# A linear-attention and feed-forward kernel on one core: another order of its steps from the 380th on

## The chip, the core and the metric

The kernel runs on one core of a Trainium2 chip. The core has five engines that run their own queues in order and wait for each other through semaphores: TensorE (PE, matrix products, written to PSUM), VectorE (DVE, elementwise work, scans and 32x32 block transposes), ScalarE (ACT, copies and activations), GpSimd (POOL) and SyncE (SP), whose queue issues all the DMAs here. The time is the device time of one execution in microseconds (us). Before the change it was 537.36 us, the median of three runs (537.22 to 537.84).

## The reference

A recurrent gated linear attention runs over 4 batches, 8 heads, 768 tokens and head dimension 48; its output, 3072 tokens of 384 values, goes through a feed-forward block with a hard-swish and a hidden width of 2048:

```python
for t in range(S):
    state = alpha[:, :, t, :, None] * state + np.einsum('bhd,bhe->bhde', k[:, :, t], v[:, :, t])
    y[:, :, t] = np.einsum('bhd,bhde->bhe', q[:, :, t], state)
x = y.transpose(0, 2, 1, 3).reshape(B * S, H * D)
h = x @ w_in
g = h * np.clip(h + 3.0, 0.0, 6.0) / 6.0
out = g @ w_out
```

## The kernel before, in words

**Attention.** The sequence is cut into 24 chunks of 128 tokens (six for each batch, numbered 0 to 23). For chunk j the steps load alpha, k, q and v (`la`, `lk`, `lq`, `lv`), bring alpha, k and q into the layout with channels on partitions (`ca`, `tk`, `tq`; from chunk 6 on a DVE block transpose of four loads, L286), run one scan backwards for the decay to the chunk's end with a reciprocal (`r`, L309) and one forwards (`p`, L320), and multiply k and q by them (`k`, `q`, L332). `sc` are the chunk's scores on PE (L346), `m` masks them on DVE in four operations (L356), `qa` lets ACT place q beside them (L366). From chunk 8 on k comes into the layout by token through DRAM: DVE turns blocks (`kt`, L391), four DMAs write them (`kw`, L396) and four read them back (`kr`, L404). `u` is k's product with v (PE, L429), `sm` adds it to the state on DVE in two halves (L437, L439), `st` decays the state on POOL (L409), and `sv` places the state beside v: two ACT copies (L419), or a POOL memset where a batch begins. `ya` and `yb` are the two halves of the output (PE, L455), and `cy` copies it to x (ACT, L464).

**Feed-forward.** Two chunks make a group of 256 tokens (0 to 11). From group 2 on the first layer is done by 20 products instead of 24, from sums of blocks: `xc` makes eleven sums of blocks of x (DVE, 128x128), `y` made the sums of the weights once (DVE, 128x512), `M.g.i` is product i (PE, four matrix products, L600), `n` copies a product from its PSUM bank to one of 16 SBUF slots (ACT, L606), and `o.g.o.0` and `o.g.o.1` put output o together on DVE (L537 to L541). `e` is the relu of the hard-swish (ACT, L494), `h` its end (DVE, L498). The second layer uses seven products instead of eight: `s` makes sums of halves of the hidden block (DVE, L647, L664), `P.g.i` is product i (PE, eight matrix products, L703), `K` keeps partial results (ACT, L682 and L709), `G` finishes a quarter of the output (two by ACT, L720, and two by DVE, L723; group 1 has three by DVE), and `O` stores it (L728). `z` are idle products. A trailing number of a step names the buffer: a PSUM bank, a slot or an output tile.

**What sets the order.** All the code runs under a manual schedule. One long string lists 1788 steps, and each step emits its instructions at once; so the string alone sets the order on every engine's queue. An engine waits at an instruction until what it reads is there and what it overwrites has been read, and everything behind it on that engine waits too. The products of one accumulating chain use the same PSUM bank, so that for example `M.g.12` may start only when `n.g.11` has copied that bank. The chunk's buffers alternate with j (two each for alpha, k, q and their results), and v has three.

```python
    def run(words):
        for word in words.split():
            name, *at = word.split(".")
            steps[name](*(int(x) for x in at))
```

Of the kernel before, what the change touches and what calls it, by code (L numbers as in the profile page):

```python
# [17 lines left out]
def kernel(  # L18
# [42 lines left out]
    G = 2  # L61
# [510 lines left out]
    for i in range(8):  # L572
        r, o = divmod(i, 3)
        spots.append(raws[r].rearrange("p n w -> p (n w)").bitcast(FP)[:, o * QB : (o + 1) * QB])
    xc = consts.tile([C, len(X_SUMS), C], FP, tag="xc")
# [178 lines left out]
    with tc.manual_schedule():  # L754
# [3 lines left out]
               dx.0 w.2 d2.2 kb.1.0 ck.1 lq.1 r.2 sm.0.1 st.1 tq.1.2 q.1 d3.2 z.0.3 d1.2 dx.2  # L758
               lv.1.1 u.1.3.1 sv.1.0 sm.1.0 p.2 sm.1.1 sc.1.0.2 m.1 ya.0.3 yb.0 cy.0 lq.2 w.1 d1.1
               tq.2.1 q.2 d4.2 lk.2 tk.2.3 k.2 fa.2.0 d4.0 st.2 sc.2.0.2 d2.1 d3.1 m.2 dx.1 d4.1  # L760
               qa.1.1 lk.3 la.3 ta.3.1 ca.3 la.4 fa.0.1 sv.1.1 w.3 r.3 ta.4.3 ca.4 r.4 tk.3.1 k.3
               kb.2.0 qa.1.0 d2.3 ya.1.2 yb.1 cy.1 fa.1.2 lq.3 ck.2 d1.3 p.3 d3.3 lv.2.2 u.2.3.2
               sm.2.0 d4.3 fb.2 tq.3.1 q.3 fb.1 qa.2.0 sm.2.1 sv.2.0 st.3 fr.0.2.0 fg.0.2 lk.4
               tk.4.0 sv.2.1 w.5 d2.5 k.4 d3.5 d1.5 qa.3.0 d4.5 qa.2.1 sc.3.1.3 m.3 w.6 d2.6 d1.6
               d3.6 d4.6 lv.3.0 lq.4 w.7 kb.3.2 fb.0 f.0.3.3 kb.4.0 ya.2.1 ck.3 u.3.3.2 sm.3.0
               fr.0.3.1 fg.0.3 fr.0.1.0 fg.0.1 qa.3.1 sv.3.0 sm.3.1 p.4 d2.7 sv.3.1 d1.7 d3.7 d4.7
               f.0.5.0 fr.0.5.1 fr.0.0.0 fg.0.5 fg.0.0 tq.4.3 ck.4 la.5 ta.5.2 f.0.6.3 ca.5 w.4
               d2.4 ya.3.0 yb.3 cy.3 fr.0.6.1 yb.2 cy.2 w.9 d2.9 q.4 qa.4.1 d1.4 d1.9 dx.4 la.6 w.8
               d3.4 r.5 lk.5 w.10 d3.9 p.5 ca.6 fg.0.6 d4.9 w.12 lq.5 lv.4.1 d2.8 d3.8 f.0.7.2 d1.8
               st.4 d4.8 d4.4 w.11 fr.0.7.0 fg.0.7 f.1.7.0 fr.1.7.1 fg.1.7 sc.4.0.2 m.4 f.1.1.1  # L770
               fr.1.1.0 fg.1.1 f.1.3.3 fr.1.3.1 d2.10 d1.10 tk.5.3 f.1.0.2 d2.12 d3.10 d4.10 w.13
               fg.1.3 fr.1.0.0 fg.1.0 k.5 d3.12 lq.6 f.1.6.0 f.1.2.1 u.4.1.0 sm.4.0 d1.12 d4.12
               sv.4.0 qa.4.0 ya.4.2 fr.1.6.1 fg.1.6 w.15 tq.5.3 fa.4.3 sv.4.1 d2.11 kb.5.1 d2.13
               fr.1.2.0 f.1.4.2 fr.1.4.1 d1.11 sm.4.1 q.5 r.6 d3.11 d3.13 fg.1.4 d4.11 lv.5.0 lk.6
               tq.6 p.6 d2.15 d3.15 fg.1.2 d1.13 d4.13 sc.5.0.3 yb.4 f.1.5.0 fr.1.5.1 fg.1.5 tk.6
               m.5 b.1.0.2 fb.4 b.1.1 d1.15 d4.15 st.5 y.5 w.14 la.7 lk.7 cy.4 d2.14 qa.5.1 ck.5
               b.0.0.1 fr.0.4.0 d3.14 k.6 q.6 ca.7 fg.0.4 d1.14 d4.14 x.0 y.1 y.10 b.0.1 y.0 y.2
               u.5.2 P.1.0.0 K.1.0 qa.5.0 sv.5.0 qa.6.1 P.1.1.3 b.0.2 b.1.2 kb.6.0 ya.5.3 y.6
               s.1.0.0 sm.5.0 sv.5.1 G.1.0.0 tk.7 s.1.1.1 s.1.2.3 x.1 yb.5 cy.5 b.1.3 sc.6.1.2
               lv.6.2 ck.6 u.6.3.0 s.1.3.2 x.2 P.1.2 b.0.3 K.1.1 y.7 s.1.4 s.1.5 y.11 y.3 r.7  # L780
               xc.2.1 x.3 y.4 y.8 xc.2.3 k.7 xc.2.0 xc.2.4 y.9 y.12 y.16 y.13 y.15 P.1.3.3 K.1.2
               P.1.4 bo.1 P.1.5 xc.2.5 G.1.1.1 P.1.6 y.14 y.17 y.19 xc.2.6 sm.6.0 G.1.2.2 y.20
               M.2.0.2 lv.12.1 la.8 O.1.1 O.1.0 ca.8 y.18 y.21 y.23 so.1 G.1.3.3 n.2.0.8 bo.0 lq.7
               lv.7.0 O.1.2 m.6 xc.2.2 xc.2.10 xc.2.7 tq.7 r.8 p.7 xc.2.8 sv.6.1 M.2.15.3 M.2.1
               kb.7.3 n.2.1.9 M.2.16 M.2.2 n.2.2.10 M.2.7.0 n.2.7.11 sm.6.1 xc.2.9 q.7 p.8 M.2.3
               M.2.4 n.2.4.12 M.2.8 o.2.0.0 M.2.5 n.2.5.13 qa.7.0 sv.6.0 st.7 lk.8 O.1.3 lq.8 lk.9
               la.9 la.10 tk.8 tq.8 lq.10 lq.9 ya.6.1 yb.6 M.2.9 z.1.3 M.2.18.1 o.2.1.0 e.2.1.1
               M.2.10 cy.6 ck.7 sc.7.0.2 u.7.1.3 n.2.10.14 M.2.11 qa.7.1 ca.9 la.11 y.22 M.2.6.2
               h.2.1 q.8 m.7 e.2.0.0 h.2.0 n.2.11.15 qa.6.0 n.2.18.10 qa.8.1 M.2.12 M.2.19
               n.2.12.12 M.2.13 sm.7.0 sv.7.1 r.9 k.8 o.2.3.0 sv.7.0 ya.7.0 y.24 o.2.5.0 n.2.13.12  # L790
               o.2.2.0 yb.7 cy.7 sc.8.1.2 xc.3.1 o.2.2.1 e.2.2.1 xc.3.3 o.2.3.1 M.2.14 xc.3.4
               xc.3.0 xc.3.5 o.2.4.0 xc.3.7 xc.3.6 o.2.6.0 P.2.0.1 M.3.0.2 M.2.17 h.2.2 o.2.6.1
               e.2.3.0 h.2.3 o.2.7.0 n.3.0.12 M.3.1 n.3.1.9 e.2.5.1 M.3.7.0 n.3.7.13 xc.3.8 o.2.7.1
               K.2.0.3 xc.3.2 kt.8 e.2.6.0 h.2.6 tk.9 M.3.2 n.3.2.10 e.2.4.0 P.2.1 h.2.4 h.2.5
               s.2.0.14 e.2.7.0 G.2.0.1 h.2.7 M.3.3 M.3.4 n.3.4.8 k.9 s.2.1.11 M.3.8 o.3.0.0 ca.10
               kt.9 P.2.3.3 s.2.2.15 s.2.3.14 lv.8.2 kw.8 kr.8 lk.10 sm.7.1 xc.3.9 M.3.5 n.3.5.11
               K.2.2 e.3.0.1 xc.3.10 M.3.9 o.3.1.0 P.2.2 K.2.1 u.8.0.3 M.3.18.2 s.2.5 M.3.10
               n.3.10.14 n.3.18.15 e.3.1.0 s.2.4 P.2.4 tq.9 h.3.0 st.8 sv.8.0 M.3.11 n.3.11.8 tk.10
               p.9 sm.8.0 q.9 r.10 k.10 qa.9.0 qa.9.1 m.8 sm.8.1 h.3.1 M.3.19 o.3.5.0 kt.10 P.2.5
               G.2.2.0 st.9 M.3.12 sc.9.0.1 qa.8.0 n.3.12.10 o.3.3.0 kw.9 lv.9.0 kr.9 sv.8.1  # L800
               u.9.2.3 sm.9.0 sv.9.1 sv.9.0 G.2.1.2 sm.9.1 st.10 M.3.15.2 M.3.16 M.3.6.3 M.3.13 m.9
               o.3.4.0 o.3.6.0 tq.10 n.3.13.10 o.3.2.0 e.3.4.1 ya.8.2 yb.8 ya.9.3 yb.9 cy.9 M.3.14
               M.3.17 cy.8 xc.4.1 P.2.6 e.3.5.0 G.2.3.3 o.3.2.1 xc.4.3 h.3.4 xc.4.4 o.3.6.1 xc.4.5
               xc.4.0 xc.4.6 e.3.2.1 M.4.0.0 n.4.0.10 P.3.0.1 xc.4.7 o.3.7.0 p.10 h.3.5 o.3.3.1
               xc.4.8 M.4.7.3 M.4.1 xc.4.2 h.3.2 o.3.7.1 K.3.0.2 lk.11 O.2.2 tk.11 e.3.6.0 e.3.3.1
               h.3.3 P.3.1 e.3.7.1 n.4.1.13 M.4.2 ca.11 q.10 h.3.6 r.11 k.11 h.3.7 n.4.7.15 lv.10.2
               lv.11.0 kw.10 sc.10.0.1 kr.10 G.3.0.0 u.10.3.2 sm.10.0 qa.10.1 n.4.2.14 M.4.3 M.4.4
               M.4.8 s.3.0.9 xc.4.9 s.3.2.12 s.3.1.11 P.3.3.2 n.4.4.8 M.4.5 o.4.0.0 e.4.0.0 sv.10.1
               sm.10.1 xc.4.10 kt.11 O.2.0 O.2.3 lq.11 m.10 s.3.3.9 s.3.5 M.4.9 o.4.1.0 P.3.2
               sv.10.0 st.11 n.4.5.11 K.3.2 la.13 M.4.18.0 p.11 tq.11 lk.12 tk.12 K.3.1 M.4.10  # L810
               n.4.10.9 q.11 qa.10.0 n.4.18.12 e.4.1.1 la.12 s.3.4 ca.12 h.4.0 r.12 P.3.5 G.3.2.1
               h.4.1 M.4.11 P.3.4 n.4.11.8 M.4.12 n.4.12.14 qa.11.0 M.4.19 p.12 G.3.1.3 lq.12 kw.11
               O.2.1 tq.12 kr.11 u.11.3 sc.11.0.2 sv.11.0 O.3.1 lk.13 P.3.6 qa.11.1 M.4.6.2 G.3.3.2
               k.12 o.4.3.0 m.11 sm.11.0 sv.11.1 kt.12 M.4.13 n.4.13.14 q.12 o.4.3.1 e.4.3.0
               o.4.2.0 o.4.6.0 h.4.3 o.4.2.1 ya.10.1 ya.11.0 yb.10 yb.11 cy.11 cy.10 xc.5.1 ca.13
               xc.5.3 M.4.15.1 M.4.16 M.4.14 P.4.0.2 o.4.4.0 M.4.17 xc.5.4 o.4.5.0 xc.5.0 xc.5.5
               M.5.0.0 o.4.6.1 K.4.0.3 e.4.2.1 h.4.2 P.4.1 qa.12.1 e.4.4.0 xc.5.6 o.4.7.0 h.4.4
               o.4.7.1 tk.13 n.5.0.14 M.5.1 e.4.7.1 h.4.7 e.4.5.0 xc.5.2 h.4.5 xc.5.7 G.4.0.3
               e.4.6.1 h.4.6 s.4.1.12 s.4.0.11 xc.5.8 r.13 xc.5.9 xc.5.10 k.13 kw.12 kr.12 la.14
               sc.12.2.3 u.12.0.1 sm.12.0 n.5.1.13 M.5.2 n.5.2.15 M.5.7.1 n.5.7.8 P.4.3.3 s.4.2.9  # L820
               kt.13 lk.14 lq.13 O.3.0 O.3.3 lv.13.2 kw.13 O.4.0 lq.14 tq.13 lq.15 M.5.3 M.5.4
               M.5.8 s.4.3.10 P.4.2 sv.12.1 n.5.4.11 o.5.0.0 e.5.0.0 K.4.2 s.4.5 p.13 ca.14 M.5.9
               M.5.5 n.5.5.12 m.12 sm.12.1 o.5.1.0 q.13 P.4.5 K.4.1 G.4.2.0 qa.12.0 qa.18.0 s.4.4
               h.5.0 M.5.18.0 n.5.18.9 o.5.6.0 tk.14 qa.13.0 M.5.10 n.5.10.10 M.5.15.3 M.5.16
               M.5.11 M.5.19 r.14 k.14 n.5.11.11 o.5.7.0 kr.13 u.13.0.2 sc.13.1.3 M.5.12 P.4.4
               e.5.1.1 n.5.12.9 M.5.13 h.5.1 o.5.4.0 m.13 o.5.5.0 st.13 sv.13.0 ya.13.1 qa.13.1
               e.5.4.0 n.5.13.15 sm.13.0 sv.13.1 h.5.4 la.15 ca.15 sv.12.0 ya.12.3 yb.12 cy.12
               yb.13 cy.13 kt.14 G.4.1.2 tq.14 M.5.14 o.5.6.1 M.5.6.0 xc.6.1 o.5.3.0 xc.6.3 o.5.2.0
# [110 lines left out]
```

## Time and profile before

| | before |
|---|---|
| median of 3 runs | 537.36 us |
| the profiled execution | 537.71 us, of which its span is 535.56 us |
| PE busy, matrix products / weight loads | 523.6 us (98%) / 497.0 us (93%) |
| DVE busy | 475.1 us (89%) |
| ACT busy | 259.7 us (48%) |
| POOL busy | 50.4 us (9%) |
| granted TensorE clock | 1.00 |

The span runs from the first to the last instruction; the rest of the execution's time lies around it. Matrix products are pipelined, and the ends of their records are modelled, so PE's busy share alone doesn't say how full PE is; the distance from one start to the next does. DVE's records overlap by a little where one follows another without a wait. A wait is put down to the engine whose signal came last. In a timeline line the columns are the start, the length, the engine, the line of the kernel, the operation, what is written and read, how many instructions are merged, and in brackets the idle time ahead of it with what ended it. In a line of busy times by stretch the length is followed by the busy time of PE, of its weight loads, of DVE, ACT and POOL with their instruction counts, the granted clock, the share of the DMA engines and GB/s.

### The profile page before, as it was taken

What the parts mean: (1) busy time and instruction counts of PE and PEld (TensorE: products, weight loads), DVE (VectorE), ACT (ScalarE), POOL (GpSimd) and SP (SyncE); (2) the same over time, 40 slices, a digit from 0 to 9 for tenths busy, and PEclk for the clock granted to TensorE, in tenths of its full rate; (3) what the DMA queues carried; (4) which work ended last, traced back from release to release, by engine and by line L of the source; (5) the groups of instructions that cost most, each with busy time, mean ns of one, the idle gap of its engine ahead of it and who ended that gap; (6) DMA issues with size and microseconds to landing.
All of it is one profiled execution on the core that took longest, in us unless ns stands there. A gap on an engine that the chain in (4) does not pass through costs nothing.

```text
span 535.6 us, 15166 instructions
## 1 busy us (share of the span) xinstructions
PE 523.6 (98%) x6306; PEld 497.0 (93%) x6306; DVE 475.1 (89%) x839; ACT 259.7 (48%) x513; POOL 50.4 (9%) x71
## 2 busy tenths in 40 slices
PE   7799999999999999999999999999999999999997
PEld 7698886789999999999999999999999999999996
DVE  6999989999999899989999899999999898595381
ACT  3889864302753644543644444642634545553240
POOL 5333435000000000000010000000000000000000
PEclk9999999999999999999999999999999999999999
DMA  9998877006515155254354355055354042100001
GB/s 175 214 250 263 205 218 164 9 1 162 151 28 121 29 120 134 51 139 90 92 118 104 89 122 141 20 126 124 85 137 103 17 97 48 43 3 1 15 16 37
DMA packets 124100, 54.40 MB, mean 102 GB/s; under 512 B 83328, under 2 KB 116864, under 8 KB 124032
## 3 DMA queue, kind: packets, MB, share of 16 engines
q1 hardware_dynamic: 124032, 53.44, 42.4%
q8 instruction: 49, 0.80, 0.7%
q14 instruction: 19, 0.16, 0.1%
HBM read 44.50 MB, written 8.91 MB: 100 GB/s over the span
## 4 chain that ended last, share of the span: by engine, by line
PE 64%; DVE 20%; SPq 5%; DMA 3%; issue 3%; ACT 2%; POOL 2%; DVEq 0%; ACTq 0%; POOLq 0%
PE m_ps L703 28%; PE m_ps L600 24%; PE m_ps L478 4%; SPq L262 3%; PE t_ps L455 3%; DVE R L309 2%; DVE g_sb L498 2%; DVE A L356 2%; DMA v<-in_v_dram 1%; PE t_ps L346 1%; PE m_ps L516 1%; PE t_ps L429 1%; DVE g_sb L537 1%; DVE q L332 1%; DVE t L286 1%
## 5 line engine op out<-in xcount | busy, mean ns | idle before, releaser
L703 PE MATMUL m_ps<-w,g_sb 128*128 128x192 f32 x704 | 122.1, 327 | 0.7 <-ACT m_ps L709 0.6
L606 ACT COPY g_sb<-m_ps 128x512 f32<-128x512 f32 x110 | 63.5, 584 | 113.8 <-PE m_ps L600 97.4
L703 PEld LDWEIGHTS m_ps<-w,g_sb 128*128 128x128 f32 x704 | 113.7, 190 | 1.8 <-ACT m_ps L709 0.9
L703 PE MATMUL m_ps<-rings,g_sb 128*128 128x192 f32 x528 | 91.6, 327 | 0.6 <-ACT u L682 0.6
L703 PEld LDWEIGHTS m_ps<-rings,g_sb 128*128 128x128 f32 x528 | 85.3, 190 | 1.0 <-ACT u L682 0.9
L600 PE MATMUL m_ps<-xc,w 128*128 128x128 f32 x640 | 82.8, 277 | 0.5 <-DVE w L541 0.5
L600 PEld LDWEIGHTS m_ps<-xc,w 128*128 128x128 f32 x640 | 77.5, 192 | 1.7 <-issue 0.6
L494 ACT ACTIVATE r<-g_sb,half 128x512 f32<-128x512 f32 x80 | 56.7, 722 | 29.5 <-DVE g_sb L541 11.7
L498 DVE SCALAR_TENSOR_TENSOR g_sb<-r,g_sb 128x512 f32<-128x512 f32 x80 | 53.6, 683 | 7.2 <-ACT r L494 6.8
L600 PE MATMUL m_ps<-xT,raw 128*128 128x128 f32 x400 | 52.6, 278 | 1.0 <-ACT g_sb L606 0.9
L600 PEld LDWEIGHTS m_ps<-xT,raw 128*128 128x128 f32 x400 | 48.6, 192 | 2.0 <-ACT g_sb L606 1.4
L409 POOL TENSOR_TENSOR st<-sm,R 128x192 f32<-128x192 f32 x20 | 12.9, 644 | 354.4 <-DVE sm L439 305.6
L647 DVE TENSOR_TENSOR g_sb<-g_sb 128x512 f32<-128x512 f32 (+1 forms) x55 | 42.0, 792 | 1.4 <-PE m_ps L703 1.1
L600 PE MATMUL m_ps<-xT,w 128*128 128x128 f32 x320 | 42.0, 276 | 0.0
L600 PEld LDWEIGHTS m_ps<-xT,w 128*128 128x128 f32 x320 | 39.3, 192 | 0.1
L366 ACT COPY A<-q 48x256 f32<-48x256 f32 x88 | 35.6, 404 | 4.9 <-DVE q L332 3.7
L356 DVE TENSOR_TENSOR A<-t_ps,mask 64x256 f32<-64x256 f32 x96 | 36.0, 413 | 0.4
L478 PE MATMUL m_ps<-xT,w 128*128 128x256 f32 x144 | 32.8, 382 | 0.1
L600 PE MATMUL m_ps<-xc,raw 128*128 128x128 f32 x240 | 31.8, 276 | 0.0
L309 DVE TENSOR_TENSOR_SCAN R<-t,ones 128x516 f32<-128x516 f32 x24 | 29.6, 1235 | 1.1 <-ACT t L300 1.0
L478 PEld LDWEIGHTS m_ps<-xT,w 128*128 128x128 f32 x144 | 26.7, 190 | 3.8 <-POOL w L217 0.2
L600 PEld LDWEIGHTS m_ps<-xc,raw 128*128 128x128 f32 x240 | 29.6, 192 | 0.1
(105 smaller groups left out, 724.8 us busy)
## 6 DMA issues: line engine op xcount, KB each, us to landing
raw<-in_moe_w_out_dram SPq DMA_DIRECT2D x8, 768.0 KB, 5.2
raw<-in_moe_w_in_dram SPq DMA_DIRECT2D x6, 768.0 KB, 6.7
v<-in_v_dram SPq DMA_DIRECT2D x48, 96.0 KB, 3.0
out_dram<-oh SPq DMA_DIRECT2D x44, 96.0 KB, 1.7
far<-kq SPq DMA_DIRECT2D x64, 64.0 KB, 2.2
kb<-far SPq DMA_DIRECT2D x64, 64.0 KB, 2.0
aq<-in_alpha_dram SPq DMA_DIRECT2D x36, 96.0 KB, 2.4
qq<-in_q_dram SPq DMA_DIRECT2D x36, 96.0 KB, 2.4
```

What stands on the lines that cost most here:

```text
L262: nc.sync.dma_start(out=to[BLK * o : BLK * (o + 1), :, 0 : V * D - skip], in_=t[o // 2, :, :, skip : V * D])
L309: nc.vector.tensor_tensor_scan(out=reverse(R, n - 1, n), data0=reverse(ax, n, n), data1=reverse(ones, n, n), initial=0.0, op0=ALU.mult, op ...
L356: nc.vector.tensor_tensor(out=to[:, a], in0=sc[a][half], in1=mask[half, half].unsqueeze(1).to_broadcast([HB, NP, HB]), op=ALU.mult)
L366: nc.scalar.copy(out=to[:, a], in_=Q_t[j][64 * a : 64 * a + D, :, half])
L455: nc.tensor.matmul(y_of(j, (i + 1) // 2, p)[:, HB * b : HB * b + HB], vb[:, p, e : e + 32], A_t[j][:, b, 2 * p + a], start=(b == 0 and i = ...
L478: nc.tensor.matmul(h[:, f], w1[:, kk, o : o + C], xT_t[g][:, kk], start=(kk == 0), stop=(kk == KT - 1))
L494: nc.scalar.activation(out=to, in_=h, func=AF.Relu, bias=half, scale=1.0 / 6.0)
L498: nc.vector.scalar_tensor_tensor(out=to, in0=r, scalar=1.0, in1=h, op0=ALU.min, op1=ALU.mult)
L600: nc.tensor.matmul(acc[g][i][:, f * C : (f + 1) * C], spots[w][:, f * C : (f + 1) * C], x_of(g, x), start=(first and f == 0), stop=last, s ...
L606: nc.scalar.copy(out=slots[z], in_=acc[g][i])
L647: nc.vector.tensor_tensor(out=out, in0=in0, in1=in1, op=ALU.subtract)
L703: nc.tensor.matmul(to[g], a, rhs[:, f], start=(first and f == 0), stop=(last and f == HF - 1), skip_group_check=True)
```

## The change

The string of steps is written anew from its 380th word on (the first one that differs; counted from 0). The 380 steps ahead of it are unchanged, though their lines break in other places. The steps behind it are the same 1408 with the same buffer numbers, in another order, which was found by a search over a replay of the program; the replay counts the fetching of instructions, and engines that hold each other up. The core of the diff:

```diff
-               P.1.4 bo.1 P.1.5 xc.2.5 G.1.1.1 P.1.6 y.14 y.17 y.19 xc.2.6 sm.6.0 G.1.2.2 y.20
-               M.2.0.2 lv.12.1 la.8 O.1.1 O.1.0 ca.8 y.18 y.21 y.23 so.1 G.1.3.3 n.2.0.8 bo.0 lq.7
-               lv.7.0 O.1.2 m.6 xc.2.2 xc.2.10 xc.2.7 tq.7 r.8 p.7 xc.2.8 sv.6.1 M.2.15.3 M.2.1
-               kb.7.3 n.2.1.9 M.2.16 M.2.2 n.2.2.10 M.2.7.0 n.2.7.11 sm.6.1 xc.2.9 q.7 p.8 M.2.3
...
-               p.9 sm.8.0 q.9 r.10 k.10 qa.9.0 qa.9.1 m.8 sm.8.1 h.3.1 M.3.19 o.3.5.0 kt.10 P.2.5
-               G.2.2.0 st.9 M.3.12 sc.9.0.1 qa.8.0 n.3.12.10 o.3.3.0 kw.9 lv.9.0 kr.9 sv.8.1
...
-               lv.11.0 kw.10 sc.10.0.1 kr.10 G.3.0.0 u.10.3.2 sm.10.0 qa.10.1 n.4.2.14 M.4.3 M.4.4
...
-               M.5.5 n.5.5.12 m.12 sm.12.1 o.5.1.0 q.13 P.4.5 K.4.1 G.4.2.0 qa.12.0 qa.18.0 s.4.4
...
-               yb.13 cy.13 kt.14 G.4.1.2 tq.14 M.5.14 o.5.6.1 M.5.6.0 xc.6.1 o.5.3.0 xc.6.3 o.5.2.0
...
-               e.5.5.0 p.15 h.5.5 M.6.1 P.5.1 G.5.0.1 n.6.1.13 M.6.2 n.6.2.14 sc.14.0.3 lv.14.0
...
-               xc.8.6 M.8.0.3 n.8.0.11 e.7.3.1 tq.18 xc.8.2 r.19 q.18 P.7.0.0 xc.8.7 h.7.3 xc.8.8
...
-               n.10.2.14 h.9.4 h.9.5 K.9.0.3 e.9.7.1 h.9.7 e.9.6.0 h.9.6 s.9.0.13 P.9.1 sm.22.1
...
-               s.11.3.9 P.11.3.2 K.11.0.0 s.11.2.14 P.11.2 o.11.3.1 K.11.2 o.11.2.1 e.11.2.0 h.11.2
-               s.11.4 e.11.3.1 h.11.3 P.11.1 G.11.0.2 s.11.5 O.11.0 K.11.1 P.11.4 G.11.1.0 P.11.5
-               G.11.2.1 O.11.2 P.11.6 G.11.3.2 O.11.1 O.9.2 O.11.3""")
...
+               y.9 y.12 y.16 y.13 y.15 P.1.3.3 K.1.2 P.1.4 bo.1 P.1.5 xc.2.5 G.1.1.1 P.1.6 y.14 y.17
+               xc.2.6 lq.7 la.8 sm.6.0 y.18 y.19 sv.6.1 sv.6.0 y.20 M.2.0.2 sm.6.1 xc.2.7 y.21
+               G.1.2.2 so.1 n.2.0.8 y.23 bo.0 M.2.15.3 M.2.1 M.2.16 n.2.1.9 lq.8 ca.8 lk.8 M.2.2
+               G.1.3.3 n.2.2.10 la.10 xc.2.2 xc.2.8 tq.7 m.6 M.2.7.0 la.9 kb.7.3 p.7 n.2.7.11 lk.9
...
+               P.2.6 n.3.13.10 e.3.4.1 M.3.14 G.2.3.3 o.3.2.0 o.3.7.0 lq.12 xc.4.0 kt.10 h.3.4
+               o.3.2.1 xc.4.4 P.3.0.1 o.3.6.1 xc.4.5 e.3.2.1 h.3.2 xc.4.6 M.4.0.0 e.3.6.0 lv.10.2
+               o.3.3.1 e.3.3.1 lq.11 xc.4.8 la.13 O.2.1 M.3.17 h.3.6 kw.10 xc.4.7 n.4.0.10 sv.10.0
+               M.4.7.3 h.3.3 lk.12 o.3.7.1 M.4.1 kr.10 K.3.0.2 r.11 n.4.7.15 O.2.3 tk.11 P.3.1
+               s.3.0.9 e.3.7.1 h.3.7 n.4.1.13 M.4.8 k.11 kt.11 q.10 kw.11 M.4.2 tq.11 lk.13 G.3.0.0
+               u.10.3.2 n.4.2.14 ca.12 s.3.2.12 sc.10.0.1 M.4.3 M.4.4 n.4.4.8 s.3.1.11 tk.12 P.3.3.2
...
+               n.5.4.11 P.4.2 p.13 k.14 st.13 xc.5.9 s.4.5 ca.15 M.5.5 q.13 kr.13 kt.14 sv.12.1
+               o.5.0.0 lq.15 m.12 K.4.1 P.4.5 lk.15 s.4.4 M.5.9 sc.13.1.3 o.5.1.0 n.5.5.12 tk.15
+               G.4.2.0 lq.14 sv.13.0 m.13 u.13.0.2 M.5.10 M.5.18.0 e.5.0.0 M.5.15.3 n.5.10.10 M.5.11
...
+               xc.6.0 G.4.3.3 h.5.3 kt.15 e.5.5.0 K.5.0.3 M.6.1 n.6.1.13 h.5.6 e.5.7.1 la.18 P.5.1
+               p.15 h.5.5 kw.15 h.5.7 xc.6.7 M.6.2 M.6.7.2 n.6.2.14 s.5.1.11 n.6.7.8 sc.14.0.3 r.16
+               xc.6.8 lv.18.2 q.15 p.16 u.14.1.2 M.6.8 sv.14.0 kr.15 s.5.0.15 ca.18 G.5.0.1 qa.14.1
...
+               M.7.17 r.20 xc.8.2 u.18.0.3 lv.19.0 xc.8.6 n.8.0.11 h.7.3 sc.18.1.2 e.7.2.0 la.22
...
+               kr.22 xc.10.6 O.8.3 xc.10.10 n.10.0.8 M.9.17 qa.22.0 h.9.4 M.10.1 h.9.2 o.9.7.1
+               K.9.0.3 e.9.3.0 n.10.1.9 h.9.3 e.9.7.1 tk.23 e.9.6.0 M.10.7.2 P.9.1 qa.22.1 u.22.2.3
...
+               h.11.6 s.11.0.11 s.11.1.8 G.10.3.0 e.11.2.0 h.11.2 s.11.2.14 K.11.0.0 o.11.3.1
+               s.11.3.9 e.11.3.1 O.10.3 O.10.1 P.11.3.2 s.11.4 P.11.2 h.11.3 K.11.2 P.11.1 K.11.1
+               P.11.4 s.11.5 G.11.0.2 G.11.1.0 P.11.5 G.11.2.1 O.11.0 P.11.6 O.11.2 O.11.1 G.11.3.2
```

## The prediction

> **What bounds the kernel.** I read the page's first part, then each engine's busy time by stretch, then what TensorE (PE) and VectorE (DVE) waited for behind the first moved step, then single places in the timeline. The change begins at step 380; the first PE step behind it, M.2.0.2, starts at 125.4 us.
>
> ```profile
> PE 523.6 (98%) x6306; PEld 497.0 (93%) x6306; DVE 475.1 (89%) x839; ACT 259.7 (48%) x513; POOL 50.4 (9%) x71
> ```
>
> Busy time by stretch from there on (length, then each engine's busy time):
>
> ```profile
> 125.40:180.00 54.60, 53.97 (x676) 52.37 (x678) 53.41 (x98) 28.85 (x61) 2.40 (x3) 1.00 0.44 103
> 180.00:246.00 66.00, 65.83 (x894) 64.29 (x893) 61.59 (x116) 31.59 (x68) 1.03 (x2) 1.00 0.40 94
> 246.00:346.00 100.00, 99.10 (x1233) 97.38 (x1232) 94.99 (x170) 47.93 (x102) 4.87 (x7) 1.00 0.43 102
> 346.00:440.00 94.00, 94.00 (x1264) 92.33 (x1263) 88.99 (x165) 41.52 (x88) 2.35 (x4) 1.00 0.42 97
> 440.00:536.00 96.00, 91.61 (x872) 90.27 (x870) 58.34 (x104) 36.14 (x74) 0.52 (x1) 1.00 0.09 26
> ```
>
> PE is nearly full throughout; DVE is the second limit: 98% busy up to 180, 95% from 246 to 346, 61% at the end, where no attention is left. So PE decides the end, and the order can only win what PE waits:
>
> ```profile
> PE m_ps L600 <- ACT g_sb L606: 0.9, 1, 0.9
> PE m_ps L703 <- ACT u L682: 0.6, 1, 0.6
> PE m_ps L703 <- ACT m_ps L709: 0.6, 2, 0.4
> PE m_ps L600 <- DVE w L541: 0.5, 1, 0.5
> ```
>
> These five waits, 2.6 us, are all that the waits view has for PE behind 125.4 us. The rest of PE's time there is work that no order removes: M steps 0.89 us apart, P steps 2.60, and some 0.2 us for each of the 30 excursions from M and P into the small attention products and back, of which the new order also has 30. What DVE waited for, from 125.4 to 354 us (sum, times, longest), shows the other side:
>
> ```profile
> DVE g_sb L498 <- ACT r L494: 4.2, 5, 1.5
> DVE oh L723 <- ACT A L366: 1.4, 1, 1.4
> DVE xc L537 <- ACT xT L464: 1.0, 1, 1.0
> DVE g_sb L537 <- PE m_ps L600: 0.9, 2, 0.6
> DVE g_sb L537 <- ACT g_sb L606: 0.9, 1, 0.9
> ```
>
> With two short ones that is 9.0 us in 12 waits; up to 254 us it is 4.9 us in 6.
>
> **The change part by part.** No instruction is added or removed, and every buffer number is kept; 1,369 of the 1,408 steps from the 380th on change place, half of them by 12 places or more.
>
> *The five waits.* (1) M.2.1 waits 0.47 for y.23. Between y.17 and y.23 DVE loses ca.8 (0.95 by start to start) and gains sm.6.1 and xc.2.7 (0.27 + 0.20); y.23 comes some 0.5 sooner: gain 0.47, and M.2.16's inputs are next and ready. (2) M.6.2 at 281.35 waits 0.90 for ACT's copy n.6.1.13, which stood behind G.5.0.1, and that needs P.5.1's end:
>
> ```profile
> 280.49 0.32 ACT L720 COPY oh<-m_ps 128x192 f32<-128x192 f32 x1 [1.94 <-PE m_ps L703]
> 280.71 0.59 ACT L606 COPY g_sb<-m_ps 128x512 f32<-128x512 f32 x1
> 281.35 0.97 PEld L600 LDWEIGHTS m_ps<-xT,raw 128*128 128x128 f32 x8 [1.19 <-ACT g_sb L606]
> ```
>
> Now n.6.1.13 stands ahead of P.5.1 and G.5.0.1 behind M.6.8: gain 0.90. (3) P.9.1 at 444.07 waits 0.45 for K.9.0.3, which stood behind n.10.2.14; now it stands behind M.10.1: gain 0.45. (4) P.11.4 waits 0.63 for K.11.1, which stood behind G.11.0.2 and so waited for P.11.1 without need:
>
> ```profile
> 524.03 0.32 ACT L720 COPY oh<-m_ps 128x192 f32<-128x192 f32 x1 [3.65 <-PE m_ps L703]
> 524.24 0.33 ACT L682 COPY u<-m_ps 128x192 f32<-128x192 f32 x1
> ...
> 524.62 2.57 PEld L703 LDWEIGHTS m_ps<-rings,g_sb 128*128 128x128 f32 x16 [0.93 <-ACT u L682]
> ```
>
> Now K.11.1 comes first: gain 0.63; s.11.5 (1.4 on DVE) then lies under P.11.4's 2.60. (5) P.2.1's 0.16 goes, as its copy K.2.0.3 gets a longer lead. Sum: 2.61, of which 0.63 lies up to 255 us, 0.90 at 281 and 1.08 behind 440.
>
> *What is paid.* DVE's attention steps move ahead. I take the work that stands ahead of a pair, DVE's producer and PE's consumer, by each form's start-to-start time (a 512-wide operation recorded at 0.68 us starts 0.60 after its predecessor). At M.5.10, which needs the bank that o.5.1.0 frees, PE has the same work ahead as before (0.02 more), DVE one chunk's preparation more: kt 0.63, tk 0.95, ca 0.95, q 0.60, r 1.35, k 0.58, and s.4.4 1.13: 6.2. Before, o.5.1.0 ended at 253.72 and M.5.10 started at 254.98: 1.26 of lead. If DVE fills all 6 waits up to there it wins their 4.9 and some 0.08 of overlap each, 5.4: the lead becomes 1.26 - 6.2 + 5.4 = 0.5. At M.8.1 (which needs xc.8.6) DVE has 10.4 more ahead (tk, ca, kt, k, p, two each of r, q, tq, xc) and PE 1.7 less (a P step fewer, one u and one sc more); lead before 358.23 - 353.83 = 4.4; 12 waits filled are 10.0: 4.4 - 10.4 - 1.7 + 10.0 = 2.3. Behind 440 DVE runs at 61% and binds nothing.
>
> So what counts is how much DVE still idles in the new order; call it y. No view of before shows it. Below, y is 0. Above, the full stretch up to 180 idled 1.19 of 54.6 us, 2.2%: y = 2.8 by M.5.10 and 5.0 by M.8.1. What speaks for the lower half: a wait of DVE for ACT's relu (0.72) comes where little DVE work stands between o and h of one output; in groups 2 to 8 five such places have 1.3 us or less between (h.4.1, h.4.7, h.3.2, h.3.3, h.4.5), against 0.72 and ACT's queue; at some 0.2 us each that is 1.0, and the other hand-overs perhaps 0.2 to 0.7. I take y = 1.2 by M.5.10 and 1.7 by M.8.1. Then PE is 1.2 - 0.5 = 0.7 later than before at M.5.10 (the 0.63 won is lost there too), wins 0.90 at M.6.2 (0.2 ahead), is not held at M.8.1 (2.3 - 1.7 = 0.6), and wins 1.08 at the end: 1.3 in all.
>
> *DMAs.* Loads (la, lk, lq, lv) and stores move by up to 371 places on SP's queue; DVE waited for no load in before (its list names no DMA), and the loads' buffers come free earlier with the transposes that read them: 0; if one came late, DVE would wait and y grow. The trip of k through DRAM tightens: between kt.10 and u.10.3.2 PE's work ahead less DVE's was 18.7 us and is 8.9. From kt's end to the last kr issue the shortest trip took 6.27, landing 2.0; lk.12's four issues (1.9) now stand in it, and kt is 0.6: 10.8. PE was 4.3 behind its bare sum at that place and DVE some 1 without its waits: 8.9 + 3.3 = 12.2. Covered by 1.4, for u.9 by about 2; if that cover is gone, PE waits first behind u.10, and sc.10 is queued behind it. Bounds 0 and 1.7 (two trips as long as chunk 15's, 7.11); I take 0, the nearer row. POOL's memsets for chunks 12 and 18 move to idle POOL time: 0. The tail's last store still follows G.11.3.2: 0.
>
> *Locks.* POOL's decayed state meets DVE:
>
> ```profile
> L409 POOL TENSOR_TENSOR st<-sm,R x20: 506/516/1477, 20.0 to 448.0; 128x192 f32<-128x192 f32 x20
> ```
>
> It took 1.48 under a scan, and twice (332.8, 390.8) the DVE operation beside it came 0.32 late. Bounds for 16 of these in the new order: 0.64 as now (change 0) to 16 x 0.32 = 5.1 (change 4.5 in y). I take 0, since 14 of the 16 held nothing. The Trainium skill, "SBUF — State Buffer", section "SBUF: two separate sides", says that GpSimd and a DVE operation with two SBUF inputs lock each other out of a shared port pair for the whole instruction; a DVE with fewer gaps would then meet more locks, and by that rule the sum moves towards the upper end.
>
> **The rivals.** (a) y near 0: 0.5 by M.5.10 and then 0.90 and 1.08, 2.5 us, are won: 534.9. For it: most hand-overs in the new order have work between. Against: no stretch of before had it. (b) y between 2 and 4: at 3 by M.8.1 PE is 0.7 late there and wins 1.08 later, 537.0. For it: the 2.2% above; against: fewer tight hand-overs than waits of before. (c) The other side: DVE becomes the bound. At y = 5.0 M.8.1 is 5.0 - 2.3 = 2.7 late, 1.08 comes back: 1.6 slower, 539.0. It is slower by over 0.2% from y = 4.5 on. For it: DVE's and ACT's queues are in order, so one late relu holds copies behind it for which PE waits. Against: ACT is 48% busy. (d) The k trip costs 1.4 + 1.2: 538.6. (e) The locks at their upper end: 1.7 + 4.5 - 2.3 = 3.9 late, less 1.08: 540.2.
>
> **How the numbers follow.** The profiled execution took 537.71 us (span 535.56), 0.35 over the median of 537.36; differences are taken off the median. Forecast: 537.36 - 1.3 = 536.1. About 0.2%, 1.07 us, is what a measurement can tell from no change. Chances: the forecast (535.3 to 536.3) 0.34; (a) 0.12; (b) 0.26; (c) 0.17; (d) 0.05; (e) 0.06. Faster 0.46, same 0.26, slower 0.28. The range takes in (a) and (c) with a little beyond each, 534.3 to 539.4; the forecast's own is 535.3 to 536.3.
>
> **What would show it.** PE's waits for ACT L606, L682 and L709 listed above are gone; DVE's busy time up to 246 us is above 97% and its waits up to 354 us sum to under 2.5 us; M.5.10 starts near 255.0 and P.11.1 about 1 us sooner than 521.23. Wrong if DVE's waits up to 354 us stay above 4 us, if new PE waits for DVE lines L498, L537 or L647 appear between 180 and 350, or if u (L429) waits for the reads of kb.

## The result, and the profile after

The changed kernel took 536.25 us (median of 14 runs, 536.00 to 537.51), the kernel before beside it 537.50 us (median of 14, 537.15 to 537.92): the ratio is 0.9978 with a 95% interval of 0.9970 to 0.9987, 1.2 us. The forecast was 536.1. The profiled execution of the changed kernel took 536.57 us, with a span of 534.8. The size is right; most of this document is about how it came out, because between the two ends it did not follow the prediction's path.

The unchanged 380 steps ahead of the change end at 125.4 us in one profile and 125.8 in the other; over all twelve profiled executions told of here M.2.0.2 starts between 125.15 and 125.92. So I compare from there on: from the start of M.2.0.2, the first moved step of PE, to the start of P.11.6, the last product. Called *the PE stretch* below, it was 404.50 us and is 403.32: 1.18 shorter.

What PE waited for from 125.4 us on, in the changed kernel (sum in us, times, longest):

```profile
PE m_ps L600 <- DVE g_sb L537: 0.8, 1, 0.8
PE m_ps L600 <- DVE xc L537: 0.4, 1, 0.4
PE m_ps L600 <- DVE xc L539: 0.3, 1, 0.3
```

All five waits of before, 2.6 us, are gone. In their place stand three others, 1.5 us, and all three are for DVE; four of the five before were for ACT. The same view for DVE, from 125.4 to 354 us:

```profile
DVE g_sb L498 <- ACT r L494: 0.2, 1, 0.2
```

That is all that is left of 9.0 us in 12 waits; the list leaves out pauses under 0.15 us. The busy times of that whole part, of before and then of after (length, PE, weight loads, DVE, ACT, POOL, each with its instruction count, granted clock, DMA share, GB/s):

```profile
125.40:354.00 228.60, 226.90 (x2968) 221.83 (x2967) 217.86 (x401) 110.38 (x234) 8.30 (x12) 1.00 0.42 100
```

```profile
125.40:354.00 228.60, 227.07 (x2967) 221.74 (x2966) 226.13 (x410) 112.14 (x234) 7.82 (x12) 1.00 0.46 108
```

DVE was 95% busy there and is 98.9%: 8.3 us of its work came forward from behind 354, as the prediction reckoned. Of its 10.7 us without work 2.5 are left, nearly all of it in pauses too short for the list. So up to 354 us the changed kernel has two full engines.

Where PE is held shows sharper in its weight loads than in its products. In the timeline of the weight loads a line's bracket tells how long the loads had stood still and what ended it. The changed kernel's brackets above 0.3 us:

```profile
136.55 0.97 PEld L600 LDWEIGHTS m_ps<-xc,w 128*128 128x128 f32 x8 [0.97 <-DVE g_sb L537]
...
192.39 0.97 PEld L600 LDWEIGHTS m_ps<-xc,raw 128*128 128x128 f32 x8 [0.33 <-DVE xc L539]
194.80 1.86 PEld L600 LDWEIGHTS m_ps<-xc,w 128*128 128x128 f32 x16 [0.55 <-DVE xc L537]
...
313.03 0.97 PEld L600 LDWEIGHTS m_ps<-xc,raw 128*128 128x128 f32 x8 [0.51 <-DVE xc L539]
```

These are M.2.9, M.4.0.0, M.4.7.3 and M.7.0.2. At the first, o.2.0.0 frees the bank that M.2.9 needs, and DVE came to it late:

```profile
134.62 1.15 DVE L286 STREAM_TRANSPOSE k<-kq 128x512 f32<-128x512 f32 x1
135.81 0.69 DVE L537 TENSOR_TENSOR g_sb<-m_ps,g_sb 128x512 f32<-128x512 f32 x1
```

The transpose is the attention step tk.8, put right ahead of o.2.0.0; before the change it stood behind it. At the other end of the span the change did what the diff says. ACT's copies there are now (L682 is K.11.1, L720 is G.11.0.2):

```profile
521.53 0.32 ACT L682 COPY u<-m_ps 128x192 f32<-128x192 f32 x1 [2.21 <-PE m_ps L703]
524.13 0.32 ACT L720 COPY oh<-m_ps 128x192 f32<-128x192 f32 x1 [2.28 <-PE m_ps L703]
```

and PE runs through, P.11.4 at 523.93 following P.11.1 at 521.33 by 2.60 us, where it was 3.39 (521.23 to 524.62).

### The profile page after: what moved, and what is told of

The parts are those of the page before. It is cut to its first block, busy times and chain, and to the rows that moved or that the text cites. A ratio compares the mean times of both kernels' runs of the same rounds, so it can differ in the third digit from the quotient of the medians.

```text
span 534.8 us, 15117 instructions
## 1 busy us (share of the span) xinstructions
PE 523.7 (98%) x6306; PEld 496.4 (93%) x6306; DVE 475.9 (89%) x839; ACT 261.6 (49%) x513; POOL 50.6 (9%) x71
## 4 chain that ended last, share of the span: by engine, by line
PE 68%; DVE 19%; DMA 4%; SPq 4%; issue 3%; POOL 1%; ACT 0%; DVEq 0%; ACTq 0%; POOLq 0%
PE m_ps L703 27%; PE m_ps L600 23%; PE m_ps L478 6%; PE m_ps L516 4%; DVE g_sb L498 3%; PE t_ps L455 3%; DMA v<-in_v_dram 3%; SPq L262 2%; DVE g_sb L537 2%; PE t_ps L429 2%; PE t_ps L346 2%; DVE g_sb L647 2%; DVE A L356 1%; DVE q L286 1%; PE m_ps L489 1%
## 5 line engine op out<-in xcount | busy, mean ns | idle before, releaser
L606 ACT COPY g_sb<-m_ps 128x512 f32<-128x512 f32 x110 | 63.8, 586 | 107.8 <-PE m_ps L600 80.7
L600 PEld LDWEIGHTS m_ps<-xT,w 128*128 128x128 f32 x320 | 39.3, 192 | 0.5 <-ACT g_sb L606 0.2
L537 DVE TENSOR_TENSOR g_sb<-g_sb 128x512 f32<-128x512 f32 x40 | 26.9, 681 | 7.5 <-ACT g_sb L606 7.4
```

Source lines behind the costliest of these rows:

```text
L537: eng.tensor_tensor(out=out, in0=in0, in1=in1, op=ALU.add if s1 > 0 else ALU.subtract)
L600: nc.tensor.matmul(acc[g][i][:, f * C : (f + 1) * C], spots[w][:, f * C : (f + 1) * C], x_of(g, x), start=(first and f == 0), stop=last, s ...
L606: nc.scalar.copy(out=slots[z], in_=acc[g][i])
```

## The experiments

All of them are edits of the order alone, or add work to it. The theory: PE's waits that go are won; what DVE has to do earlier is paid where DVE has no idle time left. The rivals are named in each expectation. One table first; the PE stretch is compared with that of before (negative is shorter), and the last column is what lies around the span, the median of time less span, with its range (the runs' spans are recorded to a tenth, so it is good to 0.05 us). For the kernel before this is 1.73 to 1.96 us in nearly all of its runs.

| kernel | PE stretch | median us | ratio to before, 95% | around the span |
|---|---|---|---|---|
| changed kernel | -1.18 | 536.25 | 0.9978 (0.9970 to 0.9987) | 1.81 (1.74 to 1.84) |
| b_n61 | -1.18 | 536.19 | 0.9978 (0.9970 to 0.9987) | 1.78 (1.73 to 2.18) |
| b_tail | -0.90 | 537.28 | 0.9994 (0.9985 to 1.0003) | 2.40 (1.74 to 2.97) |
| a_notail | -0.20 | 537.28 | 0.9997 (0.9988 to 1.0005) | 1.78 (1.75 to 1.85) |
| b_y23 | -0.06 | 537.52 | 1.0002 (0.9993 to 1.0010) | 1.82 (1.74 to 2.61) |
| a_fix | -1.14 | 536.42 | 0.9982 (0.9973 to 0.9991) | 1.82 (1.76 to 1.86) |
| a_dve | +2.02 | 539.43 | 1.0040 (1.0028 to 1.0053) | 1.75 (1.74 to 1.83) |
| b_dve | +0.82 | 538.34 | 1.0020 (1.0011 to 1.0029) | 1.78 (1.73 to 2.19) |
| b_fixes | -2.55 | 535.52 | 0.9966 (0.9955 to 0.9978) | 2.41 (1.80 to 2.69) |
| b_two | -1.67 | 535.84 | 0.9972 (0.9960 to 0.9983) | 1.80 (1.77 to 1.82) |
| h_tail | -2.56 | 534.91 | 0.9953 (0.9940 to 0.9967) | 1.83 (1.76 to 2.35) |

### One copy earlier, in the order of before

```diff
-               e.5.5.0 p.15 h.5.5 M.6.1 P.5.1 G.5.0.1 n.6.1.13 M.6.2
+               e.5.5.0 p.15 h.5.5 M.6.1 n.6.1.13 P.5.1 G.5.0.1 M.6.2
```

> The kernel before with one edit: the copy n.6.1.13 is ahead of P.5.1 and G.5.0.1, so that M.6.2 does not wait the 0.90 us at 281.35. Theory (what is won on PE is kept as far as DVE has idle time to follow): between 281 and 354 DVE of before idles 3.5 us and its tightest results lie 0.8 us ahead of PE (s.5.1.11 for P.5.3.3 0.88, s.5.3.15 for P.5.2 0.84), so 0.6 to 0.9 us faster, ratio 0.9985. Rival (the middle of the span gives everything back, as the changed kernel gave back its lead between 275 and 345): 0 to 0.3 us.

It won 1.18 us, as much as the whole change, with one step moved. ACT's copies in the kernel before and in this one, timeline (L720 is G.5.0.1, L606 n.6.1.13):

```profile
280.49 0.32 ACT L720 COPY oh<-m_ps 128x192 f32<-128x192 f32 x1 [1.94 <-PE m_ps L703]
280.71 0.59 ACT L606 COPY g_sb<-m_ps 128x512 f32<-128x512 f32 x1
```

```profile
278.50 0.57 ACT L606 COPY g_sb<-m_ps 128x512 f32<-128x512 f32 x1
280.55 0.32 ACT L720 COPY oh<-m_ps 128x192 f32<-128x192 f32 x1 [1.47 <-PE m_ps L703]
```

The copy now runs while P.5.1 is still going. The gain was kept to the end, as the theory has it, because DVE of before had idle time behind 281 with which to follow (its listed waits up to 354 us are 8.1 us here, 9.0 before). It was larger than the 0.90 that PE's list of waits names. This is what the kernel before shows at M.6.2, once by the products and once by the weight loads:

```profile
281.35 1.16 PE L600 MATMUL m_ps<-xT,raw 128*128 128x128 f32 x8 [0.90 <-ACT g_sb L606]
```

```profile
281.35 0.97 PEld L600 LDWEIGHTS m_ps<-xT,raw 128*128 128x128 f32 x8 [1.19 <-ACT g_sb L606]
```

The weight loads stood still for 1.19 us, and 1.18 were won. The Trainium skill, "Perfetto Trace Analysis", section "Identifying the Most-Contended Engine", says that matmul busy time is a poor measure of TensorE's headroom and weight loads a good one, since the products are pipelined; these runs bear that out for single waits too: the 0.90 is counted from the modelled end of the product before, which reaches 0.17 us beyond the start that the next product would have had (P steps start 2.60 us apart and are recorded at 2.77). The other 0.11 is the head start that the loads have over their products in unbroken running (277.58 against 277.69 at P.5.1) and had lost behind the wait, where both start at 281.35.

### The tail

```diff
-               s.11.4 e.11.3.1 h.11.3 P.11.1 G.11.0.2 s.11.5 O.11.0 K.11.1 P.11.4
+               s.11.4 e.11.3.1 h.11.3 P.11.1 K.11.1 G.11.0.2 s.11.5 O.11.0 P.11.4
```

> The kernel before with one edit: the copy K.11.1 is ahead of G.11.0.2 on ACT, as in the changed kernel. Theory (the sum of the prediction): P.11.4 no longer waits the 0.63 us at 524.62, and only P.11.5 and P.11.6 follow, so 0.6 to 0.7 us faster than before, ratio 0.9987. Rival 1 (the changed tail owes its gain to the whole new order of the last 30 us): 0 to 0.2 us. Rival 2 (G.11.0.2, now later, holds the last store): 0 or slower.

> The changed kernel with one edit: G.11.0.2 is back ahead of the copy K.11.1 on ACT, as before the change. Theory: P.11.4 waits again, 0.6 to 0.7 us slower than the changed kernel, so 0.5 to 0.7 us faster than before, ratio 0.9989. Rival (the other moves of the tail cover K.11.1): no slower than the changed kernel, ratio 0.9977.

On PE the two edits are mirror images. The order of before with K.11.1 first has a PE stretch 0.90 us shorter; the changed kernel with G.11.0.2 first again has one 0.99 longer than the changed kernel (-0.20 against -1.18). In that kernel the wait is back to the hundredth, timeline of the weight loads:

```profile
524.28 1.76 PEld L703 LDWEIGHTS m_ps<-rings,g_sb 128*128 128x128 f32 x11 [0.93 <-ACT u L682]
```

So the theory's 0.63 was too small for the same reason as at M.6.2 (the loads stood still for 0.93), and the other moves of the tail don't cover K.11.1. But the times don't mirror each other: a_notail lost all that the changed kernel had won, while b_tail won next to nothing, because in 10 of its 12 runs more than 1.85 us, up to 2.97, lay around its span. Two kernels further down look into that.

### One step of DVE later, in the order of before

```diff
-               M.2.0.2 lv.12.1 la.8 O.1.1 O.1.0 ca.8 y.18 y.21 y.23 so.1
+               M.2.0.2 lv.12.1 la.8 O.1.1 O.1.0 y.18 y.21 y.23 ca.8 so.1
```

> The kernel before with one edit: ca.8 (1.10 us on DVE) is behind y.23, so that M.2.1 does not wait the 0.47 us at 127.84. Theory (DVE has no idle time between 125.4 and 156, and o.2.0.0 lies 0.09 us ahead of M.2.9 at 136.7): the 0.47 us come back as a wait of M.2.9 for o.2.0.0, the time is the same within 0.15 us. Rival (each wait that goes is won, as the prediction's sum has it): 0.47 us faster, ratio 0.9991.

The wait of M.2.1 went and nothing was won: 0.06 on PE, the time the same. The theory held, though it named only the second of two steps. By M.2.4 PE was 0.66 us ahead of before; 0.43 of it went at M.2.8, which now waits for xc.2.8, and most of the rest at M.2.9, whose weight loads stood still for 0.25 us. The first of the two:

```profile
134.03 1.13 PE L600 MATMUL m_ps<-xc,raw 128*128 128x128 f32 x8 [0.26 <-DVE xc L539]
```

DVE has no listed wait between 125.4 and 156 in either kernel. There a wait of PE for DVE only changes its place when DVE's steps change theirs; a wait for ACT, as at M.6.2, can go.

### The changed kernel's new waits taken away

```diff
-               M.2.3 tk.8 lv.7.0 M.2.4 n.2.4.12 qa.7.1 M.2.8 o.2.0.0
+               M.2.3 lv.7.0 M.2.4 n.2.4.12 qa.7.1 M.2.8 o.2.0.0 tk.8
...
-               M.3.17 h.3.6 kw.10 xc.4.7 n.4.0.10
+               M.3.17 xc.4.7 h.3.6 kw.10 n.4.0.10
...
-               h.6.2 P.5.6 xc.7.5 sm.15.1
+               xc.7.5 h.6.2 P.5.6 sm.15.1
```

> The changed kernel with its three new waits of PE for DVE taken away (1.48 us in all): tk.8 (1.15 us on DVE) behind o.2.0.0, which M.2.9 waits for; xc.4.7 ahead of h.3.6, for M.4.7.3; xc.7.5 ahead of h.6.2, for M.7.0.2. DVE's work is the same. Theory (DVE is the bound of the changed kernel from 125 to 354: it waits 0.2 us there, and its results lie 0.05 us ahead of PE at M.3.9, M.4.0.0, M.5.10 and M.8.0.3 too): the waits come back at these, 0 to 0.5 us faster than the changed kernel, ratio to before 0.9968 to 0.9978. Rival (three separate misplacings): 1.2 to 1.5 us faster than the changed kernel, ratio 0.995.

All three waits went, and the PE stretch is 0.05 us longer than without the edits. The first came back 2 us later, one DVE step on: M.2.10 now waits for o.2.1.0, which stands behind tk.8 and tq.8. Weight loads, timeline:

```profile
138.66 0.97 PEld L600 LDWEIGHTS m_ps<-xc,w 128*128 128x128 f32 x8 [0.66 <-DVE g_sb L541]
...
192.20 0.97 PEld L600 LDWEIGHTS m_ps<-xc,raw 128*128 128x128 f32 x8 [0.37 <-DVE xc L539]
...
329.67 0.97 PEld L600 LDWEIGHTS m_ps<-xc,w 128*128 128x128 f32 x8 [0.33 <-DVE g_sb L537]
```

From P.6.0.1 to M.7.5 (313 to 328 us) this kernel was 0.6 us ahead of the changed one; at P.6.2 it was level, held there and at M.7.9 (the last of these lines). That is what it means that DVE is the bound: the rival, three separate misplacings, is out.

### 3.1 us more work on DVE

```diff
-               s.5.5
+               s.5.5 xc.6.2 xc.6.2 xc.6.2 xc.6.2 xc.6.2 xc.6.2 xc.6.2 xc.6.2 xc.6.2 xc.6.2
```

> The changed kernel with 2.0 us more work on DVE at 290: xc.6.2 is done ten times again behind s.5.5 (0.2 us each, the same values into the same place). Theory (DVE is the bound up to 354): its next results lie 0.76 us (xc.6.10), then 0.05 us (xc.7.5) ahead of PE and DVE has no idle time before 354, so 1.8 to 2.1 us slower than the changed kernel, ratio to before 1.0015. Rival (DVE and PE merely touch at a few places, the later order has room): up to 1 us slower than the changed kernel, ratio below 0.9997.

> The kernel before with the same 2.0 us more work on DVE behind s.5.5 (292 there). Theory (before, DVE is not the bound): 1.39 us of it fill the idle time that ends at 297.84, the rest is inside the 1.11 us that xc.7.5 lies ahead of M.7.0.2, and 1.09 us more idle time ends at 325.24: 0 to 0.4 us slower, ratio 1.0000 to 1.0008. Rival (both kernels are bound by DVE alike): 1.5 to 2 us slower, ratio 1.003 to 1.004.

The ten repeats took not 2.0 us but 3.14, since each sum that overwrites the place the one before it wrote started 0.33 us after it, not 0.20. DVE in the kernel before with them:

```profile
292.56 3.23 DVE L537 TENSOR_TENSOR xc<-xT 128x128 f32<-128x128 f32 x10
295.70 1.11 DVE L286 STREAM_TRANSPOSE k<-kq 128x512 f32<-128x512 f32 x1
```

In the changed kernel 3.14 us of DVE cost 3.21 us of PE, all of it (+2.02 against -1.18), at once at M.6.10 and then at M.7.0.2:

```profile
295.17 1.16 PE L600 MATMUL m_ps<-xc,w 128*128 128x128 f32 x8 [2.22 <-DVE xc L537]
315.57 1.16 PE L600 MATMUL m_ps<-xc,raw 128*128 128x128 f32 x8 [0.72 <-DVE xc L539]
```

In the kernel before the same 3.14 cost 0.82 us of PE, and its list of PE's waits has no new line. The idle time of 1.39 us that ended at 297.84 took up part of it. What PE lost it lost ahead of M.7.0.2, which the expectation had in view: 0.55 us between M.6.13 and M.6.6.1, where the outputs (L455) stand and need the state that DVE's `sm` makes and ACT copies, and 0.10 at M.6.12. Weight loads of that kernel:

```profile
308.52 0.64 PEld L455 LDWEIGHTS t_ps<-A,v 128*32 128x32 f32 x32 [0.25 <-ACT v L419]
```

So both expectations fell by their numbers, having the dose wrong, and the theory stands: the change turned DVE from an engine with room into the bound of this part.

### Three copies, and then two

```diff
-               M.6.1 P.5.1 G.5.0.1 n.6.1.13 M.6.2
+               M.6.1 n.6.1.13 P.5.1 G.5.0.1 M.6.2
...
-               sm.22.0 n.10.2.14 h.9.4 h.9.5 K.9.0.3 e.9.7.1
+               sm.22.0 K.9.0.3 n.10.2.14 h.9.4 h.9.5 e.9.7.1
...
-               P.11.1 G.11.0.2 s.11.5 O.11.0 K.11.1 P.11.4
+               P.11.1 K.11.1 G.11.0.2 s.11.5 O.11.0 P.11.4
```

> The kernel before with three edits: n.6.1.13 ahead of P.5.1, K.9.0.3 ahead of n.10.2.14, K.11.1 ahead of G.11.0.2; three ACT copies that PE waited for, 1.98 us in all. Theory (a gain is kept where DVE can follow): 0.8 for M.6.2, 0.1 of the 0.45 us at P.9.1 (s.9.1.12 for P.9.3.3 lies 0.11 us ahead), 0.65 at P.11.4, together 1.4 to 1.7 us, ratio 0.9971: as fast as the changed kernel or faster, with three of its 1408 moves. Rival 1 (each wait is won in full): 2.0 us, ratio 0.9963. Rival 2 (the new order as a whole is needed, single moves give theirs back): below 1.0 us.

On PE it won 2.55 us, more than either theory said: 1.18 at M.6.2, 0.49 at P.9.1 (where I had expected 0.1; the weight loads had stood still for 0.57) and 0.90 at P.11.4. The first and the last are those of the single edits, and P.9.1's is also the difference between b_n61 and the next kernel, so nothing was given back. In time it won 1.86, since 2.41 us lay around the span. The next two tell the tail apart:

> The kernel before with n.6.1.13 ahead of P.5.1 and K.9.0.3 ahead of n.10.2.14, and with K.11.1 where it was. The runs with K.11.1 moved in the order of before won 0.9 us in the span, but 0.6 us of it were gone in what lies around the span (2.4 us in the middle, not 1.78). Theory 1 (that edit in that code brings the time around the span): the span gives 1.19 for M.6.2 and 0.48 for P.9.1, around the span stay 1.75 to 1.85 us, together 1.65 us faster, 535.7 us, ratio 0.9969. Theory 2 (the earlier end brings it, whatever the edit): around the span above 2 us, about 536.3 us, ratio 0.998.

Without the edit to K.11.1 (the first two pieces of the diff alone), the PE stretch is 1.67 shorter and 1.80 lies around the span, with no run above 1.82. Theory 1 held: the higher median around the span comes with K.11.1's new place in the tail of before.

The last kernel has the same two edits, and its last 88 steps (from the 1700th on) stand in the order of the changed kernel. The end of that part:

```diff
...
-               P.11.1 G.11.0.2 s.11.5 O.11.0 K.11.1 P.11.4 G.11.1.0 P.11.5 G.11.2.1 O.11.2
-               P.11.6 G.11.3.2 O.11.1 O.9.2 O.11.3""")
+               P.11.1 K.11.1 P.11.4 s.11.5 G.11.0.2 G.11.1.0 P.11.5 G.11.2.1 O.11.0 P.11.6
+               O.11.2 O.11.1 G.11.3.2 O.9.2 O.11.3""")
```

> The same two edits, and the last 88 of the 1788 steps in the order of the changed kernel, K.11.1 ahead of G.11.0.2 among them. The span should be that of the kernel with three edits, 533.4 us. Theory 1 (the time around the span grew by how that edit stands among the other steps of the tail before; the changed kernel has the same edit and 1.74 to 1.84 us): around the span 1.8 us, 535.1 to 535.2 us, ratio 0.9958. Theory 2 (it is the shorter time between two waits of one engine, as in the changed order, but with the length of the code before): 2.4 us, 535.6 us, ratio 0.9967.

534.91 us, 0.9953 of before (0.9940 to 0.9967), is the best of all, 1.3 us below the changed kernel. Its PE stretch is that of b_fixes, and around the span lie 1.83 us, with one run of five at 2.35; so theory 1 held again. What is left of PE's waits:

```profile
PE m_ps L600 <- DVE w L541: 0.4, 1, 0.4
PE m_ps L703 <- ACT m_ps L709: 0.2, 1, 0.2
```

Its part from 246 to 346 us, with the room on DVE that the changed kernel (98.56 of 100) no longer has there:

```profile
246.00:346.00 100.00, 100.00 (x1243) 98.57 (x1242) 95.98 (x173) 48.92 (x104) 4.87 (x7) 1.00 0.44 103
```

## Why the prediction was right, and where it was not

**The five waits.** All five went, as forecast, but their sum of 2.61 us was mis-sized. Alone, M.6.2 was worth 1.18, not 0.90; P.9.1 0.49, not 0.45 (by difference); P.11.4 0.90, not 0.63; and M.2.1 0.06, not 0.47. The prediction quoted the weight loads' lines at M.6.2 and P.11.4, with 1.19 and 0.93 in their brackets, and took the smaller numbers of the products.

**y, DVE's idle time.** The prediction put y at 1.2 by M.5.10 and 1.7 by M.8.1 and wanted it from waits for the relu. That step failed: the list has one such wait, of 0.2 us. By the list y is near 0, the condition of rival (a), for which the prediction had 534.9 us; the time stayed 1.3 above that, since the sum that y enters was off as well. Filling the 12 waits did not win the 10.0 us it has: DVE's time without work fell by 8.3, as short pauses stay and add up. Counted from M.2.0.2, o.5.1.0 ended 1.14 us later than before, where the sum has 0.8 + y: in effect y was 0.3. xc.8.6 ended 2.30 later, where it has 0.4 + y: in effect 1.9, near the 1.7 that was taken, but for other reasons.

**What is paid.** The prediction weighed two pairs, M.5.10 with o.5.1.0 and M.8.1 with xc.8.6. It made PE 0.7 us late at the first; M.5.10 started 0.07 us earlier than before, counted from M.2.0.2, with o.5.1.0 just 0.06 ahead of it. At the second it came close: M.8.1 was to start 1.9 us sooner (1.7 of that less work ahead) and started 1.81 sooner, with xc.8.6 0.28 us ahead of it where 0.6 was forecast. (The work ahead is 1.5 less by the distances of before, 2.60 for P.7.0.0 less 1.08 for u.18 and sc.18, so PE was 0.3 ahead.) But PE was held by DVE on the way, at M.2.9, M.4.0.0, M.4.7.3 and M.7.0.2, which were not looked at, by 2.36 us of standing weight loads in the four lines shown. So the price of DVE's full queue was foreseen, and its places and its form were not: not one long wait at the end of the lead, but several, where the order inside DVE's queue happens to put other work ahead of what PE needs. a_fix shows that moving the places wins nothing, and a_dve that the price is real.

**The sum.** At steps of PE that have the same PE work behind them in both orders, their starts can be compared. The lead of the changed kernel over before, counted from M.2.0.2:

| step | us in before | lead, us |
|---|---|---|
| M.2.8 | 134 | 0.50 |
| M.2.6.2 | 142 | -0.30 |
| M.4.1 | 195 | -0.42 |
| P.4.3.3 | 242 | 0.32 |
| M.6.0.1 | 272 | 0.20 |
| P.5.3.3 | 286 | 1.14 |
| M.7.1 | 318 | 0.57 |
| P.7.1 | 362 | 0.29 |
| P.9.0.1 | 436 | -0.22 |
| P.9.2 | 452 | 0.29 |
| P.11.1 | 521 | 0.29 |
| P.11.4 | 525 | 1.08 |
| P.11.6 | 530 | 1.19 |

So M.2.1 was won and lost again at M.2.9. Between 195 and 242 it was the kernel before that lost more, in pieces too short for its list. M.6.2 was won and for the most part lost to DVE before 362. P.9.1 was won after as much had been lost in small pieces behind 370; their cause stays open. P.11.4 makes up most of the result (0.99, as a_notail shows). The prediction won too little and paid too little, and the errors nearly cancelled: 1.3 forecast, 1.2 measured. That the size agrees so well is luck.

**DMAs and the k trip.** Costed at nothing, they cost next to nothing: the list of PE's waits has no line for u (L429). The cover came out near the sums: chunk 10's reads had landed 1.6 us ahead of u.10 (1.4 forecast), chunk 9's 1.4 ahead of u.9 (about 2); the tightest was 0.5, at u.18. Rival (d) fell.

**Locks.** Here the term that was put at no change was not nothing, though small. DVE's operations that run beside POOL's decayed state are at times longer. In before three were, by 0.20, 0.30 and 0.31 us (the prediction saw the last two); in the changed kernel five are, by 0.32 each, and behind 125 us no other DVE operation in either kernel runs over 0.12 us longer than is usual for its form. One of the five; the usual length of this sum is 0.68:

```profile
447.54 0.80 POOL L409 TENSOR_TENSOR st<-sm,R 128x192 f32<-128x192 f32 x1 [19.68 <-DVE sm L439]
...
447.88 1.00 DVE L647 TENSOR_TENSOR g_sb<-g_sb 128x512 f32<-128x512 f32 x1
```

That is 1.6 us against 0.8; but up to 354 us, where DVE is full, 0.6 against 0.5, so rival (e) fell. The Trainium skill's rule in "SBUF — State Buffer", section "SBUF: two separate sides", would have a fuller DVE meet more locks; the trace agrees in that, and the sum stayed far below the upper end.

**What would show it.** PE's waits for ACT L606, L682 and L709 are gone (right); DVE is above 97% up to 246 us and waits under 2.5 us up to 354 (right: 54.06 of 54.60 up to 180, 65.61 of 66.00 from there, and 0.2 us); M.5.10 near 255.0 (right only by the weak word); P.11.1 about 1 us sooner than 521.23 (wrong: 521.33, or 0.3 sooner counted from M.2.0.2). A new wait of PE for DVE L537 between 180 and 350 was on the list of what would make it wrong; it is there at 194.80, with 0.35 us.

## What to carry to other kernels

Before moving hundreds of steps, look at each wait of the bounding engine and ask whether the engine it waits for has idle time: a copy on a half-idle engine that stands behind one that can't start yet is won by moving that one step, and is kept where the other engines have room to follow; a wait for an engine that is itself full only moves. Price a wait of TensorE by how long its weight loads stood still, not by the gap between products. And an order that fills the second engine's last idle time has spent the cover of everything behind it: two copies moved by themselves, with the new tail, gave twice the gain of the whole new order.

## What the runs showed of the hardware that I had not expected

- On DVE a 128x128 sum that writes where the one just before it wrote started 0.33 us after it (the ten repeats). The same holds for a sum that reads what the one just before it wrote: seven such pairs of `xc` in before are 0.31 to 0.33 us apart, twelve in the changed kernel 0.31 to 0.40. Two sums without such a tie are 0.18 to 0.21 us apart (25 pairs in before, 22 after). So the order of the sums alone can cost or save some 0.12 us for each.
- A DVE operation beside POOL's decayed state took up to 0.32 us longer than usual, as told above.
- The time around the span is no constant. It is 1.73 to 1.85 us in most runs, but up to 2.97 where K.11.1 was moved in the tail of before (and 2.61 in one run of b_y23, which leaves the tail alone). Of the twelve profiled executions two show a fetch of instructions behind the last instruction of the span, 16 KB each: that of before (2.15 us around its span) and that of b_tail (2.57). The ten others, 1.77 to 1.81 us, show none. The DMA view of b_tail from 535 us on, 0.1 us behind the end of its span:

```profile
DMA packets 1, 0.02 MB, mean 2 GB/s; under 512 B 0, under 2 KB 0, under 8 KB 0
## 3 DMA queue, kind: packets, MB, share of 16 engines
q8 instruction: 1, 0.02, 0.6%
```

  That the fetch makes these runs longer is likely but was not shown, and why one moved copy brings it on stays open.
- Of the unchanged first 380 steps the end moved by 0.8 us from one profile to another (125.15 to 125.92), two thirds of the change's whole effect, while equal edits gave leads equal to some 0.05 us (1.17 to 1.22 at M.10.2 in the four kernels that have n.6.1.13 moved in the order of before). Where a change leaves the head alone, the difference from its first step on is the better measure.
